# Streamed operands 64 bytes further along in SBUF, in an adaLN block with linear attention and a token mixer

## The chip, the cores and the metric

One core of a Trainium2 chip runs the whole program; the other cores are idle. The metric is the time of one execution on the device in microseconds; a profile is taken of one execution. The kernel is written in Bass with the Tile framework, in an order set by hand.

## The reference, cut to what matters

All tensors are float32: x is 2048 tokens by 448 channels, wqkv 448 x 1344, wo 448 x 448, w1 2048 x 1792, w2 1792 x 2048, w_mod 448 x 2688.

```python
mod = (_silu(c) @ w_mod).reshape(c.shape[0], 6, 1, -1)
sa, ca, ga, sb, cb, gb = (mod[:, i] for i in range(6))
h = _layernorm(x) * (1 + ca) + sa
q, k, v = heads of h @ wqkv                      # 16 heads of 28 channels
pq, pk = phi(q), phi(k)                          # elu + 1
o = (pq @ (pk^T v)) / (pq . sum of pk over tokens)
x = x + ga * (o @ wo)
h = _layernorm(_layernorm(x) * (1 + cb) + sb)
u = _gelu(einsum("bsd,sf->bdf", h, w1) + b1)     # first product over tokens
y = einsum("bdf,fs->bds", u, w2) + b2            # second product over tokens
x = x + gb * transpose(y)
```

(The lines are shortened; the heads' reshapes are written in words.)

## The kernel before, in words

TensorE takes two operands per matmul: the *held* one (weights, 128 columns, loaded ahead by a LDWEIGHTS) and the *streamed* one (here up to 448 columns). To keep float32 accuracy at the rate of fp32r, the kernel cuts each float32 operand into a high and a low part, both of type fp32r: `split` (L69) copies to the high part on ScalarE (L70) and subtracts it from the whole on VectorE (L71); in some places the low part is made on ScalarE and by an accumulating DMA from GpSimd's queue instead (`w_low_dma` L186, `low` L349, `PIECE_DMA` L219). A product is then three matmuls: high x high, high x low, low x high.

Nearly all tiles lie in two pools with places of 2048 bytes: `slots` (76 places, `slot` L60) and `tok` (25 places, `tslot` L63). A tile of 448 columns fills 1792 bytes of its place. The 14 tiles `uw`, 3584 bytes each, lie in a pool `uparts` (L793), which is opened where `tok` was, once that is closed. The places of slots, tok and uparts all begin at multiples of 128 bytes.

The stages, in the order in which TensorE works:

- **Modulation and input** (to about 18 us of the span): c and w_mod, first LayerNorm.
- **Tokens, first pass** (18 to 111 us), 16 tiles of 128 tokens. `project` (L299) makes K (`kp`) and, for some tiles, Q (`qp`): it holds slices of the transposed, normalised tile (hh, hl) and streams the parts of the weights, Whi and Wlo, which lie in tok. `a_outer` (L385) holds slices of the normalised tile (xh, xl) and streams pkh and pkl, the parts of phi(k) made in `a_pk_parts` (L369), into four accumulators `cacc`. V is never made: K^T h is multiplied by the V weights afterwards (`kvb`, L594).
- **Folded output weights** (L717): kvm x wo in float32 (`wp`), cut into Wph and Wpl, which lie in tok.
- **Attention output** (128 to 215 us): the loop at L728 does, for turn i, the transposes of tile i (`tq`), the output product of tile i-1 (`b_out` L647, twelve matmuls that stream Wph and Wpl), later Q projections, statistics and normalisation of tiles i-2 to i-4 on ScalarE, VectorE and GpSimd, and a first share of the first product over tokens. `b_norm2` (L692) and `b_low2` make H2h and H2l, the parts of the twice normalised tile.
- **First product over tokens** (`up`, 156 to 325 us): `step` (L709) and `acc3` (L704) hold slices of the parts of w1 (ph, pl) and stream H2h and H2l: L705 and L707 stream the high part, L706 the low one. `finish_u` (L804) applies gelu, and writes the parts of u into uw: in two halves of 224 columns, each as high then low. `u_parts` (L799) writes sums of u's halves into ordinary slots (`ut1` to `ut4`).
- **Second product over tokens** (325 us to the end): token tiles 0 to 9 are done by Strassen's scheme, seven products for four quadrants (`mult7` L877, out `y`): L889 streams 448 columns and L890 the first 224 of a uw or a ut tile. Three of the seven stream uw, four stream ut. Tiles 10 to 15 are done in the plain form (`mult1` L937, out `yp`), which uses `acc3` again and streams two pieces of 224 columns out of uw. The list `order` (L957) interleaves the two; loads and splits are called some entries ahead.

The order on each engine is the order in which the code is written (`manual_schedule`). DMAs go out on SyncE's queue, the accumulating ones on GpSimd's.

Of the kernel before, what the change touches and what calls it, by code (L numbers as in the profile page):

```python
# [8 lines left out]
F32 = mybir.dt.float32  # L9
F32R = mybir.dt.float32r  # L10
# [4 lines left out]
P = 128  # L15
S, D, F = 2048, 448, 1792
NT = S // P
NF = F // P
G = 112
# [23 lines left out]
def block_kernel(ctx: ExitStack, tc: tile.TileContext, x, wqkv, wo, w1, b1, w2, b2, c, wmod, out):  # L43
# [16 lines left out]
    def slot(name, w=D, dt=F32, parts=P):  # L60
        return slots.tile([parts, w], dt, name=name, tag="slot", padded_shape=[P, 512])

    def tslot(name, dt=F32, parts=P, w=D):  # L63
        return tok.tile([parts, w], dt, name=name, tag="tok", padded_shape=[P, 512])

    def bank(name):
        return psum.tile([P, 512], F32, name=name, tag="bank")

    def split(full, hi, lo):  # L69
        nc.scalar.activation(hi, full, AF.Copy)  # L70
        nc.vector.tensor_sub(lo, full, hi.bitcast(F32))  # L71
# [100 lines left out]
    Whi, Wlo = {}, {}  # L172

    def w_high(j, ch):
        Whi[j, ch] = tslot(f"wh{j}_{ch}", F32R)
        nc.scalar.activation(Whi[j, ch], raw_w[j, ch], AF.Copy)

    def w_low(j, ch):
        w, r = Whi[j, ch], raw_w[j, ch]
        if ch < 3:  # L180
            Wlo[j, ch] = tslot(f"wl{j}_{ch}", F32R)
            nc.vector.tensor_sub(Wlo[j, ch], r, w.bitcast(F32))
        else:
            nc.vector.tensor_sub(w[64:128], r[64:128], w[64:128].bitcast(F32))

    def w_low_dma(j, ch):  # L186
        w, r = Whi[j, ch], raw_w[j, ch]
        if ch < 3:
            Wlo[j, ch] = tslot(f"wl{j}_{ch}", F32R)
            lo, hi = Wlo[j, ch], w  # L190
        else:
            lo = hi = w[64:128]
            r = r[64:128]
        nc.scalar.activation(lo, hi.bitcast(F32), AF.Copy, scale=-1.0)
        nc.gpsimd.dma_start(lo, r, accum_op=ALU.add)
# [4 lines left out]
    raws, parts = {}, {}  # L200
# [148 lines left out]
    def low(t, lo, full, hi):  # L349
        if t in DVE_LOW:  # L350
            nc.vector.tensor_sub(lo, full, hi.bitcast(F32))
        else:
            nc.scalar.activation(lo, hi.bitcast(F32), AF.Copy, scale=-1.0)
            nc.gpsimd.dma_start(lo, full, accum_op=ALU.add)
# [13 lines left out]

    def a_pk_parts(t):  # L369
        pk = pkf.pop(t)  # L370
        hi, lo = slot(f"pkh{t}", dt=F32R), slot(f"pkl{t}", dt=F32R)
        nc.scalar.activation(hi, pk, AF.Copy)
        low(t, lo, pk, hi)
        if t in (0, 1, NT - 1):
            pksum.append(pk)
        elif t == NT - 2:
            pksum14.append(pk)
        else:
            nc.gpsimd.dma_start(pksum[t % 2], pk, accum_op=ALU.add)
        pks[t] = (hi, lo)  # L380
# [62 lines left out]
    a_first((2, 3))  # L443
    keep_warm(2)
    w_high(1, 0)
    a_copy((0, 1))
    a_copy((2,))
    a_copy((3,))
    del tps[0]
    st.pop(0)  # L450
    a_norm_a(1)
    w_high(1, 1)
    a_norm_b(1, sap[:, :D])
    a_dup(1)
    w_low(1, 0)
    w_high(1, 2)
    w_low(1, 1)
    kp0 = project0(1, "kp", lambda: a_transpose(1))
    a_split(1)
    w_high(1, 3)  # L460
    w_low(1, 2)
    w_low(1, 3)
    mod_out(0, sap)
# [3 lines left out]
    for ch in range(4):  # L467
        w_high(0, ch)
    a_exp(0, kp0)
    w_low_dma(0, 0)  # L470
    a_norm_b(2)
    w_low_dma(0, 1)
    a_stats(3)
    a_dup(2)
# [20 lines left out]
    a_exp(2, kp2)  # L495
    a_norm_b(4)
    a_pk_parts(0)
    a_dup(4)
    a_pk(2, kp2)
    a_phi_q()  # L500
    a_pk_parts(1)
    a_q(2)
    a_high(2)
# [6 lines left out]
    for t in range(3, NT):  # L510
# [15 lines left out]
        a_pk(t, kp)  # L526
        a_phi_q()
        a_pk_parts(t - 1)
        if t + 3 < NT:
            a_stats(t + 3)  # L530
# [14 lines left out]
        if t == 4:  # L545
            for g in range(4):
                w = tslot(f"wo{g}", parts=G)
# [58 lines left out]
    H2h, H2l = [None] * NT, [None] * NT  # L606
# [85 lines left out]
    def b_norm2(t, i):  # L692
        rs = rss[i - 1][:, 1:2]
        nb = small.tile([P, 1], F32, name=f"nb{t}", tag="nb")
        nc.gpsimd.tensor_mul(nb, nm2s.pop(t), rs)
        nc.scalar.activation(ys[t], ys[t], AF.Identity, bias=nb, scale=rs)
        H2h[t] = slot(f"h2h{t}", dt=F32R)
        H2l[t] = slot(f"h2l{t}", dt=F32R)
        nc.scalar.activation(H2h[t], ys[t], AF.Copy)

    def b_low2(t):
# [15 lines left out]
    for g in range(4):  # L717
        wp = bank(f"wp{g}")
        nc.tensor.matmul(wp[:G, :D], kvm[:, g * G:(g + 1) * G], wo_sb[g], start=True, stop=True)
        hi = tslot(f"wph{g}", F32R, G)  # L720
        lo = tslot(f"wpl{g}", F32R, G)
        split(wp[:G, :D], hi, lo)
        Wph.append(hi)
        Wpl.append(lo)
# [3 lines left out]
    for i in range(NT + LAG):  # L728
# [11 lines left out]
        t = i - LAG  # L740
# [19 lines left out]
        if norm2:  # L760
            b_norm2(i - 4, i)
# [28 lines left out]


    tok_ctx.__exit__(None, None, None)
    uparts = ctx.enter_context(tc.tile_pool(name="uparts", bufs=1, reuse_waits="tile"))  # L793
    HD = D // 2
    PAIRS, RS = NF // 2, ((0, 4), (4, 3))
# [195 lines left out]
    for o0, n in W1G[1:]:  # L991
# [5 lines left out]
        for r in range(first, NT):  # L997
# [4 lines left out]
            if xleft and k % 2:  # L1002
                t = xleft.pop(0)
# [13 lines left out]
    for n, (kind, p) in enumerate(order):  # L1017
        if jobs:
            jobs.pop(0)()
        while xleft:  # L1020
            t = xleft.pop(0)
# [40 lines left out]
```

## Time and profile before

| | |
|---|---|
| time, median of 3 runs | 458.64 us (458.63 to 460.37) |
| profiled execution, device time | 458.67 us |
| its span | 457.0 us |
| TensorE clock granted, mean | 1.00 |

In the profile, PE is TensorE's matmuls, PEld its weight loads (they run beside the matmuls), DVE VectorE, ACT ScalarE, POOL GpSimd, SP SyncE. A group of instructions has its line, engine, operation and `out<-in` by the program's tile names; a timeline row begins with start and duration in us; a row of a tile view gives minimum, median and maximum duration in ns, then the first and the last start. A row of the chain gives start and length of a piece of the chain of work that ended last. Matmuls overlap in the records: each lasts longer than the distance to the next one's start.

### The profile page before, as it was taken

Reading aid. Unit: us, or ns where it says so; the run is one execution under the profiler, and the core shown is the slowest. Engines: PE = TensorE matmul, PEld = TensorE weight load, DVE = VectorE, ACT = ScalarE, POOL = GpSimd, SP = SyncE. Lnnn points to the kernel's source line nnn. Section 1 sums busy time; section 2 is a strip of 40 time slices with the busy share of each in tenths; the row PEclk is TensorE's granted clock in tenths of the full one; section 3 lists DMA queues with packets and bytes.
Section 4 is the critical chain, followed back from the end, with each engine's and each line's share of the span. In section 5 each row is a group of like instructions: output and inputs, shape, how many; then the busy total and the mean of one; then the engine's idle time right before and its main releaser. Section 6 shows DMA issues by size and latency. Waiting matters only on the chain.

```text
span 457.0 us, 7265 instructions
## 1 busy us (share of the span) xinstructions
PE 451.6 (99%) x2378; PEld 409.9 (90%) x2378; DVE 356.7 (78%) x781; ACT 241.4 (53%) x538; POOL 90.9 (20%) x163
## 2 busy tenths in 40 slices
PE   8999999999999999999999999999999999999996
PEld 7689998998799999988999999999999999999996
DVE  5798897878898898896559676629696977798982
ACT  1648766635456576676665445226556262536350
POOL 2215675620014355554300000000000000000000
PEclk9999999999999999999999999999999999999999
DMA  8969999993200003222407453317960583628312
GB/s 228 287 174 174 172 193 227 210 226 116 70 1 2 23 24 103 61 47 48 126 17 230 162 193 106 112 39 227 288 187 23 177 239 113 176 99 250 112 55 98
DMA packets 60550, 61.85 MB, mean 135 GB/s; under 512 B 9248, under 2 KB 53856, under 8 KB 60512
## 3 DMA queue, kind: packets, MB, share of 16 engines
q1 hardware_dynamic: 54752, 52.45, 38.2%
q0 software_dynamic: 5760, 8.95, 12.0%
q8 instruction: 18, 0.29, 0.3%
q14 instruction: 20, 0.16, 0.1%
HBM read 45.09 MB, written 7.34 MB: 115 GB/s over the span
## 4 chain that ended last, share of the span: by engine, by line
PE 90%; ACT 3%; POOL 2%; DVE 1%; DMA 1%; issue 1%; SPq 1%; DVEq 0%
PE y L889 11%; PE up L705 9%; PE up L707 9%; PE up L706 9%; PE cacc L394 8%; PE kp L312 7%; PE qp L312 7%; PE y L890 5%; PE op L654 5%; PE yp L705 4%; PE yp L707 4%; PE yp L706 4%; PE tp L291 1%; DMA wm<-in_w_mod_dram 1%; PE tq L638 1%; PE modp L169 1%
## 5 line engine op out<-in xcount | busy, mean ns | idle before, releaser
L705 PE MATMUL up<-h2h,ph 128*128 128x448 f32 x224 | 82.2, 367 | 0.0
L706 PE MATMUL up<-h2l,ph 128*128 128x448 f32 x224 | 81.8, 365 | 0.0
L707 PE MATMUL up<-h2h,pl 128*128 128x448 f32 x224 | 81.8, 365 | 0.0
L71 DVE TENSOR_TENSOR pl<-pr,ph 128x512 fp32r<-128x512 f32 (+1 forms) x60 | 36.3, 615 | 13.0 <-ACT ph L70 8.3
L706 PEld LDWEIGHTS up<-h2l,ph 128*128 128x128 f32 x224 | 42.1, 188 | 3.5 <-issue 0.2
L705 PEld LDWEIGHTS up<-h2h,ph 128*128 128x128 f32 x224 | 42.1, 188 | 3.5 <-issue 0.2
L707 PEld LDWEIGHTS up<-h2h,pl 128*128 128x128 f32 x224 | 42.1, 188 | 3.4
L70 ACT ACTIVATE ph<-pr 128x512 fp32r<-128x512 f32 (+1 forms) x60 | 32.8, 567 | 16.3 <-PE up L706 11.4
L895 ACT ACTIVATE cc<-y 128x448 f32<-128x448 f32 x15 | 8.2, 545 | 56.5 <-PE y L890 39.8
L705 PE MATMUL yp<-uw,qw 128*128 128x448 f32 x84 | 31.1, 370 | 0.0
L707 PE MATMUL yp<-uw,qw 128*128 128x448 f32 x84 | 30.7, 366 | 0.0
L706 PE MATMUL yp<-uw,qw 128*128 128x448 f32 x84 | 30.7, 365 | 0.0
L394 PE MATMUL cacc<-pkh,xh 128*128 128x448 f32 x64 | 24.8, 387 | 0.0
L654 PE MATMUL op<-wph,pth 112*128 112x448 f32 x64 | 24.7, 386 | 0.0
L654 PE MATMUL op<-wpl,pth 112*128 112x448 f32 x64 | 23.4, 366 | 0.0
L394 PE MATMUL cacc<-pkl,xh 128*128 128x448 f32 x64 | 23.4, 366 | 0.0
L654 PE MATMUL op<-wph,ptl 112*128 112x448 f32 x64 | 23.4, 365 | 0.0
L70 ACT ACTIVATE qw<-q 128x256 fp32r<-128x256 f32 (+1 forms) x56 | 18.9, 352 | 7.7 <-DMA q<-in_B_w_dram 7.0
L312 PE MATMUL kp<-wh,hh 128*128 128x448 f32 x60 | 22.2, 375 | 0.0
L312 PE MATMUL qp<-wh,hh 128*128 128x448 f32 x60 | 22.2, 375 | 0.0
L810 DVE TENSOR_TENSOR u<-u,mod 128x448 f32<-128x448 f32 x14 | 8.7, 620 | 17.1 <-ACT u L809 17.1
L642 ACT ACTIVATE pth<-tq 112x512 fp32r<-112x512 f32 x16 | 9.6, 599 | 23.4 <-PE tq L638 20.4
(198 smaller groups left out, 1242.0 us busy)
## 6 DMA issues: line engine op xcount, KB each, us to landing
pr<-in_B_w_dram SPq DMA_DIRECT2D x48, 256.0 KB, 2.9
a<-in_B_w_dram SPq DMA_DIRECT2D x20, 256.0 KB, 5.2
wm<-in_w_mod_dram SPq DMA_DIRECT2D x24, 196.0 KB, 4.6
a<-in_B_w_dram SPq DMA_DIRECT2D x20, 192.0 KB, 4.9
x<-in_A_x_dram SPq DMA_DIRECT2D x16, 224.0 KB, 4.5
xpark<-x SPq DMA_DIRECT2D x16, 224.0 KB, 1.9
q<-in_B_w_dram SPq DMA_DIRECT2D x28, 128.0 KB, 3.2
xb<-xpark SPq DMA_DIRECT2D x16, 224.0 KB, 4.3
```

The source lines that it names most:

```text
L70: nc.scalar.activation(hi, full, AF.Copy)
L71: nc.vector.tensor_sub(lo, full, hi.bitcast(F32))
L312: nc.tensor.matmul(o, a[:, ch * P:(ch + 1) * P], b, start=(n == 0), stop=(n == 10))
L394: nc.tensor.matmul(cacc[ch][:, :D], a[:, s], b, start=(t == 0 and i == 0), stop=(t == NT - 1 and i == len(todo) - 1))
L642: nc.scalar.activation(phs[t][0], tps[t][:G, :], AF.Copy)
L654: nc.tensor.matmul(opb[t][:, :D], a[:, s], b, start=(n == 0), stop=(n == 11))
L705: nc.tensor.matmul(ps[:, :D], hi[:, sl], mh, start=first, stop=False)
L706: nc.tensor.matmul(ps[:, :D], hi[:, sl], ml, start=False, stop=False)
L707: nc.tensor.matmul(ps[:, :D], lo[:, sl], mh, start=False, stop=last)
L810: nc.vector.tensor_mul(u, u, mods[5])
L889: nc.tensor.matmul(ps[:, :D], h[:, s], w, start=opens and r == 0, stop=False, skip_group_check=True)
L890: nc.tensor.matmul(ps[:, :HD], l[:, s], w[:, :HD], start=False, stop=closes and r == PAIRS - 1, skip_group_check=True)
```

## The change

A helper `moving` takes a place of 512 columns and hands out columns 16 to 464 of it, so that the 448 columns begin 64 bytes into the place. All tiles that fp32r matmuls stream out of slots and tok come from it now: the parts of the QKV weights, of phi(k), of the twice normalised tiles and of the folded output weights. Ahead of the pool of the uw tiles a pool with one unused tile of 64 bytes is opened, so that every uw tile stands 64 bytes further as well. The ut tiles of `u_parts` and all held operands stay where they are. No instruction is added; the diff in full:

```diff
@@ -63,6 +63,10 @@
     def tslot(name, dt=F32, parts=P, w=D):
         return tok.tile([parts, w], dt, name=name, tag="tok", padded_shape=[P, 512])
 
+
+    def moving(new, name, dt=F32R, parts=P):
+        return new(name, dt=dt, parts=parts, w=512)[:, 16:16 + D]
+
     def bank(name):
@@ -172,13 +176,13 @@
     def w_high(j, ch):
-        Whi[j, ch] = tslot(f"wh{j}_{ch}", F32R)
+        Whi[j, ch] = moving(tslot, f"wh{j}_{ch}")
         nc.scalar.activation(Whi[j, ch], raw_w[j, ch], AF.Copy)
 
     def w_low(j, ch):
         w, r = Whi[j, ch], raw_w[j, ch]
         if ch < 3:
-            Wlo[j, ch] = tslot(f"wl{j}_{ch}", F32R)
+            Wlo[j, ch] = moving(tslot, f"wl{j}_{ch}")
             nc.vector.tensor_sub(Wlo[j, ch], r, w.bitcast(F32))
@@ -186,7 +190,7 @@
     def w_low_dma(j, ch):
         w, r = Whi[j, ch], raw_w[j, ch]
         if ch < 3:
-            Wlo[j, ch] = tslot(f"wl{j}_{ch}", F32R)
+            Wlo[j, ch] = moving(tslot, f"wl{j}_{ch}")
             lo, hi = Wlo[j, ch], w
@@ -368,7 +372,7 @@
     def a_pk_parts(t):
         pk = pkf.pop(t)
-        hi, lo = slot(f"pkh{t}", dt=F32R), slot(f"pkl{t}", dt=F32R)
+        hi, lo = moving(slot, f"pkh{t}"), moving(slot, f"pkl{t}")
@@ -694,8 +698,8 @@
-        H2h[t] = slot(f"h2h{t}", dt=F32R)
-        H2l[t] = slot(f"h2l{t}", dt=F32R)
+        H2h[t] = moving(slot, f"h2h{t}")
+        H2l[t] = moving(slot, f"h2l{t}")
         nc.scalar.activation(H2h[t], ys[t], AF.Copy)
@@ -717,8 +721,7 @@
-        hi = tslot(f"wph{g}", F32R, G)
-        lo = tslot(f"wpl{g}", F32R, G)
+        hi, lo = moving(tslot, f"wph{g}", parts=G), moving(tslot, f"wpl{g}", parts=G)
         split(wp[:G, :D], hi, lo)
@@ -790,6 +793,8 @@
     tok_ctx.__exit__(None, None, None)
+    uspace = ctx.enter_context(tc.tile_pool(name="uspace", bufs=1, reuse_waits="tile"))
+    uspace.tile([P, 16], F32, name="uspace")
     uparts = ctx.enter_context(tc.tile_pool(name="uparts", bufs=1, reuse_waits="tile"))
```

## The prediction

> **What bounds the kernel now.** I read the page's busy times first, then the chain that ended last, then single matmuls in the timeline.
>
> ```profile
> span 457.0 us, 7265 instructions
> PE 451.6 (99%) x2378; PEld 409.9 (90%) x2378; DVE 356.7 (78%) x781; ACT 241.4 (53%) x538; POOL 90.9 (20%) x163
> ...
> PEclk9999999999999999999999999999999999999999
> ...
> PE 90%; ACT 3%; POOL 2%; DVE 1%; DMA 1%; issue 1%; SPq 1%; DVEq 0%
> ```
>
> TensorE is busy 99% of the span at full granted clock and holds 90% of the chain. So the time is a sum over matmuls of the distance from one start to the next, and only something that changes that distance moves the end. The durations in the groups are longer than that distance, because matmuls are pipelined. The timeline of the first product over tokens (every line from 299.99 to 305.87 starts one matmul; 30 distances between these two and the one before) shows the distance itself:
>
> ```profile
> 299.79 0.36 PE L707 MATMUL up<-h2h,pl 128*128 128x448 f32 x1
> 299.99 0.36 PE L705 MATMUL up<-h2h,ph 128*128 128x448 f32 x1
> ...
> 305.87 0.36 PE L707 MATMUL up<-h2h,pl 128*128 128x448 f32 x1
> ```
>
> (305.87 - 299.79) / 30 = 0.2027 us for a stream of 448 columns. The chain, merged by line, shows more than one such pace, for the same eleven matmuls of the K projection in two neighbouring token tiles, and the float32 matmuls that make the folded output weights:
>
> ```profile
> 51.11 2.23 PE kp L312 x11
> ...
> 60.95 2.27 PE kp L312 x11
> ```
> ```profile
> 120.44 3.01 PE wp L719 x8
> ```
>
> 2.23 / 11 = 0.203, 2.27 / 11 = 0.206, 3.01 / 8 = 0.376. Instructions, shapes and places in SBUF modulo 2048 bytes are the same in the two kp rows; only the phase in which they follow what came before differs. A distance that has two steady values for the same work is what two streams that disturb each other would give. The float32 stream of the same 448 columns needs 0.376; if fp32r runs at twice its rate, 0.188 would be its undisturbed distance, and 0.0147 us of each 0.2027 is something else. What runs beside every matmul is the load of the next weights.
>
> ```profile
> 195.33 0.36 PE L706 MATMUL up<-h2l,ph 128*128 128x448 f32 x1
> 195.53 0.36 PE L707 MATMUL up<-h2h,pl 128*128 128x448 f32 x1
> ...
> 195.97 0.13 PEld L638 LDWEIGHTS tq<-ident,pn 128*112 128x112 f32 x1 [0.45 <-issue]
> ```
>
> The L707 at 195.53 is one of the few with no load beside it: the next one starts at 195.97, when its stream is over. Its own group, alone in the window 195.75 to 195.85, and the group of all L707 (mean in ns behind the comma):
>
> ```profile
> L707 PE MATMUL up<-h2h,pl 128*128 128x448 f32 x1 | 0.4, 360 | 0.0
> ```
> ```profile
> L707 PE MATMUL up<-h2h,pl 128*128 128x448 f32 x224 | 81.8, 365 | 0.0
> ```
>
> 360 against 365 ns: with the load beside it a stream is 5 ns longer. No other row prices the load, and I found three such matmuls in all. A second one speaks against it: the very last matmul of the kernel (plain form, no load after it), beside its group:
>
> ```profile
> L707 PE MATMUL yp<-uw,qw 128*128 128x448 f32 x1 | 0.4, 367 | 0.0
> ```
> ```profile
> L705 PE MATMUL yp<-uw,qw x84: 365/368/380, 324.9 to 452.5; 128*128 128x448 f32 x84
> L706 PE MATMUL yp<-uw,qw x84: 363/365/367, 325.1 to 452.7; 128*128 128x448 f32 x84
> L707 PE MATMUL yp<-uw,qw x84: 363/366/367, 325.3 to 452.9; 128*128 128x448 f32 x84
> ```
>
> 367 alone against a median of 366.
>
> **The change, part by part.** It adds no instruction and moves none. Slots and tok tiles are 2048 bytes apart and both pools begin at a multiple of 128 bytes; u's 3584-byte parts begin where tok began. So today every streamed operand and every weight tile of the fp32r matmuls stand a multiple of 128 bytes from each other. Afterwards the streamed one stands 64 bytes further.
>
> How many streams this reaches, from the loops: 165 kp and 165 qp (11 for each of 15 tiles), 176 cacc (11 x 16), 192 op (12 x 16), 672 up (three rows of 224), 252 yp (three of 84), and of the Strassen form the 3 of 7 products that stream uw, 35 each at L889: 105. Together 1727 streams of 448 columns. The other 140 stream ut, which u_parts keeps in plain slots; they stay.
>
> What one of them gains is shown by no row, since no fp32r pair stands 64 bytes apart. The bounds: 14.7 ns (0.2027 down to 0.188), nothing, and a loss of 3.6 ns (2.27 - 2.23 over 11, if the shift put all streams into the slower phase). I take 5 ns, the lone row, as if the shift removed what the load costs; for yp I take nothing, since its lone row shows 367. So (1727 - 252) x 5 ns = 7.4 us.
>
> [...]
>
> The short matmuls (L890, 224 columns) count nothing:
>
> ```profile
> 336.14 0.27 PE L890 MATMUL y<-uw,a11l 128*128 128x224 f32 x1
> 336.24 0.38 PE L889 MATMUL y<-uw,a11h 128*128 128x448 f32 x1
> 336.46 0.26 PE L890 MATMUL y<-uw,a11l 128*128 128x224 f32 x1
> ```
>
> L889 starts 0.10 us after L890 and shows 0.38 instead of 0.36: its weights began to load with L890 and are late, so a shorter L890 would only lengthen the wait. Bounds: 0 to 105 x 5 ns = 0.5 us.
>
> Not all of it is paid. In the attention-output stage the chain leaves TensorE:
>
> ```profile
> 175.57 0.76 ACT y L696
> ...
> 179.83 0.94 POOL pl L223
> ...
> 201.84 0.95 POOL pl L223
> ...
> 206.26 0.54 DVE pn L627
> ```
> ```profile
> 160.00:195.00 35.00, 35.00 (x185) 32.17 (x184) 30.73 (x73) 24.29 (x52) 18.98 (x40) 1.00 0.24 61
> ```
>
> From 175.57 to 206.80 the statistics, splits and accumulating DMAs of each token tile hand on to the next, and TensorE only keeps up (the figures behind the window's length are PE, PEld, DVE, ACT and POOL: DVE is busy 30.73 of 35 us). Six turns of 24 shifted matmuls lie there: 144 x 5 ns = 0.7 us are not gained, since pn would be as late as now. If this chain takes over in the whole stage (366 shifted streams from 128.5 us on), 1.8 us are lost.
>
> The writers of the shifted tiles (L70 on ACT, L71 on DVE, the accumulating DMAs on POOL's queue) write the same bytes; I cost them at nothing. Their cover: TensorE's own work, and for pkl the three tiles by which cacc follows. A DMA into pkl lands after 3.8 us,
>
> ```profile
> DMA to landing us min/median/max: 3.1/3.8/7.1
> ```
>
> and without that cover each microsecond more would be a microsecond of TensorE. The unused tile has no writer. uw3, uw7 and uw11 now reach 64 bytes into one more old tok tile (ph10, pd15, wph0), a wait for readers long gone: uw is first written at 237.1, and wph is last streamed at 214.1.
>
> ```profile
> L70 ACT ACTIVATE uw<-u x14: 558/579/581, 237.1 to 328.0; 128x448 fp32r<-128x448 f32 x14
> ```
> ```profile
> L654 PE MATMUL op<-wph,pth x64: 362/368/457, 128.5 to 214.1; 112*128 112x448 f32 x64
> ```
>
> Sum: -7.4 + 0.7 = -6.7 us. The profiled execution took 458.67 (span 457.0 and 1.67 around it), practically the median of 458.64; 458.67 - 6.7 = **452.0 us**.
>
> **The rivals.**
>
> *Nothing happens: 458.7.* For it: places that are multiples of 128 bytes apart make no difference now. L706 of yp streams from 896 bytes further into uw than L705 and L707 and lies in the same 363 to 367. And tq holds slices of pn 448 bytes apart, half of them 64 bytes off the identity that is streamed, with
>
> ```profile
> L638 PE MATMUL tq<-ident,pn x64: 270/272/295, 123.3 to 207.3; 128*112 128x128 f32 x64
> ```
>
> a median of 272 and a minimum of 270: no sign of two kinds. Against it: these stream float32 at half the rate, where 0.376 leaves room. [...]
>
> *Slower.* The shift changes the phase between stream and load, and the phase of the second kp row (0.206) becomes the rule. 1727 x 3.6 ns = 6.2 us: 464.9. Its place is every fp32r stream, and it decides as soon as the mean distance in up rises by 1.3 ns (0.5% of 458.7 us over 1727). For it: that phase exists and holds for whole runs of matmuls. Against it: 0.203 is much the commoner today, with no care for the phase.
>
> *The whole excess goes: about 439.* 14.7 ns x 1727 = 25.4 us, less the 366 streams of the attention-output stage (5.4 us), where the other engines would then set the pace. Against it: the lone matmul at 360 ns is nowhere near 14.7 ns shorter than 365. [...]
>
> *It only reaches part of the streams* lies inside the forecast's own range: half of 6.7 gives 455.3.
>
> **How the numbers follow.** Forecast 0.40 (own range 448 to 456), whole excess 0.07, nothing 0.28, slower 0.25. A difference under about 0.5% (2.3 us) can hardly be told from no change here. Faster by more than that: 0.40 + 0.07 = 0.47; within it 0.28; slower 0.25. For 8 in 10 the range leaves out the 0.07 of the whole excess and the far end of the slower case (over 466): 444 to 466.
>
> **What would show it.** Right: the median of L705 to L707 of up near 360 ns and thirty distances taking 5.9 instead of 6.08 us; kp and qp rows of the chain at 2.17 for eleven; y streaming ut unchanged while y streaming uw is shorter. Nothing: the same 365. Slower: medians of 369, eleven in 2.27 everywhere. The stage from 175 to 207 should keep its 31 us, with TensorE waiting for pn more often. The prediction is wrong if durations change by another amount than 5 ns, if yp changes where I count nothing, or if a wait on SP, ACT or DVE appears behind uw.

## The result: 2.0 us less, a third of the forecast's gain

| | median | lowest to highest | runs |
|---|---|---|---|
| before | 458.76 us | 458.63 to 460.37 | 6 |
| after | 456.75 us | 455.93 to 457.06 | 6 |

After divided by before is 0.994, 95% interval 0.9922 to 0.9959. So the kernel became 0.6% faster; the forecast had 6.7 us less (452.0), the range 444 to 466. The profiled execution of after took 457.06 us, its span 455.3.

The page of after, the lines that answer to those of before (all lines of code stand 4 further down in `acc3` and `project`: L705 to L707 are now L709 to L711, L312 is L316, L394 is L398; L889 and L890 are L894 and L895):

```profile
span 455.3 us, 7265 instructions
...
PE 448.9 (99%) x2378; PEld 409.9 (90%) x2378; DVE 356.6 (78%) x781; ACT 241.7 (53%) x538; POOL 91.6 (20%) x163
...
PE 80%; POOL 4%; ACT 4%; DVE 4%; DMA 3%; issue 3%; SPq 1%; POOLq 0%; DVEq 0%
```

The same 7265 instructions. TensorE still fills 99% of the span, but its share of the chain fell from 90% to 80%: other engines took over for some 10%. Both halves of that are the result in small: matmuls follow one another faster, and part of what they gained is waited away.

The timeline of the first product over tokens shows the faster part (every line from 296.84 to 302.64 starts one matmul; 30 distances between the first and the last row):

```profile
296.64 0.36 PE L711 MATMUL up<-h2h,pl 128*128 128x448 f32 x1
296.84 0.36 PE L709 MATMUL up<-h2h,ph 128*128 128x448 f32 x1
...
302.64 0.36 PE L711 MATMUL up<-h2h,pl 128*128 128x448 f32 x1
```

6.00 us in place of 6.08: 200.0 ns from start to start in place of 202.7. The change does what its words say, and one shifted stream gains **2.7 ns**.

Where the profiled execution lost and gained, by stage, from the starts of the stages' first matmuls (us; the attention output is counted to the start of its last `op`; the last column is 2.7 ns times the shifted streams of the stage, and a turn that ran at 206.7 ns before could give more):

| stage | before | after | difference | possible |
|---|---|---|---|---|
| start, to the first kp on split weights | 17.16 | 18.09 | +0.93 | 0 |
| tokens, first pass | 95.86 | 95.39 | -0.47 | -1.10 (407 streams) |
| kvb, folded weights, attention output | 100.38 | 99.69 | -0.69 | -1.14 (423) |
| first product (after the attention output) | 110.40 | 108.97 | -1.43 | -1.46 (540) |
| second product | 128.02 | 128.09 | +0.07 | - |

The start is not put down to the change: in both chains it hangs on a load of w_mod, which took 5.68 us in the profile of before and 6.61 in that of after, and in the eleven profiles of the block in this study the start lies between 16.93 and 18.09 us in no order that follows their code. Without it, the stages gained 2.5 us in this one execution.

Two stages kept less than was possible. The chain of waits of after, in the first pass (start, length, what), below the shares of the chain of before from 40 to 95 us, which is TensorE's alone:

```profile
by line: PE kp L312 43.8%; PE cacc L394 42.6%; PE tp L291 8.7%; PE qp L312 4.0%; PE modp L169 1.4%
```
```profile
46.83 2.20 PE kp L316 x11
...
61.38 2.21 PE kp L316 x11
63.59 0.45 PE tp L295 x4
...
64.51 0.72 POOL rs L272
...
66.58 7.55 DMA pkl<-pk
...
74.18 1.89 PE cacc L398 x8
...
76.12 0.89 POOL rs L272
...
91.15 0.54 DVE wo L560
91.69 0.61 DVE hl L75
...
92.34 2.08 PE kp L316 x9
```

Up to 64 us eleven `kp` take 2.20 to 2.21 in place of 2.23 to 2.27, and TensorE sets the pace. From there to 92 us, GpSimd and its queue, VectorE and a transfer into pkl do. In the attention output, `tq` now waits for pn (the row of the waits of PE: us in total, times, longest), which it did not before:

```profile
PE tq L642 <- DVE pn L631: 0.6, 2, 0.4
```

### The profile page after: what moved, and what is told of

It is laid out like the page before. It is cut to its first block, busy times and chain, and to the rows that moved or that the text cites. A ratio compares the mean times of both kernels' runs of the same rounds, so it can differ in the third digit from the quotient of the medians.

```text
span 455.3 us, 7265 instructions
## 1 busy us (share of the span) xinstructions
PE 448.9 (99%) x2378; PEld 409.9 (90%) x2378; DVE 356.6 (78%) x781; ACT 241.7 (53%) x538; POOL 91.6 (20%) x163
## 4 chain that ended last, share of the span: by engine, by line
PE 80%; POOL 4%; ACT 4%; DVE 4%; DMA 3%; issue 3%; SPq 1%; POOLq 0%; DVEq 0%
PE y L894 11%; PE up L711 8%; PE up L710 8%; PE up L709 8%; PE qp L316 7%; PE y L895 6%; PE cacc L398 5%; PE kp L316 5%; PE yp L709 4%; PE yp L711 4%; PE yp L710 4%; PE op L658 4%; DMA pkl<-pk 2%; DMA wm<-in_w_mod_dram 1%; ACT y L700 1%
## 5 line engine op out<-in xcount | busy, mean ns | idle before, releaser
L711 PE MATMUL up<-h2h,pl 128*128 128x448 f32 x224 | 81.3, 363 | 0.0
L709 PE MATMUL up<-h2h,ph 128*128 128x448 f32 x224 | 81.1, 362 | 0.0
L709 PEld LDWEIGHTS up<-h2h,ph 128*128 128x128 f32 x224 | 41.9, 187 | 3.1 <-issue 0.2
L711 PEld LDWEIGHTS up<-h2h,pl 128*128 128x128 f32 x224 | 42.0, 188 | 2.4
L709 PE MATMUL yp<-uw,qw 128*128 128x448 f32 x84 | 31.2, 371 | 0.0
L711 PE MATMUL yp<-uw,qw 128*128 128x448 f32 x84 | 30.6, 365 | 0.0
L398 PE MATMUL cacc<-pkh,xh 128*128 128x448 f32 x64 | 24.6, 385 | 0.0
L398 PE MATMUL cacc<-pkl,xh 128*128 128x448 f32 x64 | 23.3, 363 | 0.2 <-DMA pkl<-pk 0.2
L316 PE MATMUL kp<-wh,hh 128*128 128x448 f32 x60 | 22.0, 371 | 0.0
L316 PE MATMUL qp<-wh,hh 128*128 128x448 f32 x60 | 21.9, 371 | 0.0
L75 DVE TENSOR_TENSOR qw<-q,qw 128x256 fp32r<-128x256 f32 (+1 forms) x56 | 18.9, 352 | 3.8 <-ACT qw L74 3.8
L316 PE MATMUL kp<-wh,hl 128*128 128x448 f32 x60 | 21.7, 366 | 0.1
```

The source lines that it names most:

```text
L316: nc.tensor.matmul(o, a[:, ch * P:(ch + 1) * P], b, start=(n == 0), stop=(n == 10))
L398: nc.tensor.matmul(cacc[ch][:, :D], a[:, s], b, start=(t == 0 and i == 0), stop=(t == NT - 1 and i == len(todo) - 1))
L709: nc.tensor.matmul(ps[:, :D], hi[:, sl], mh, start=first, stop=False)
L711: nc.tensor.matmul(ps[:, :D], lo[:, sl], mh, start=False, stop=last)
```

## The experiments

Three theories stood against each other. **Distance**: what matters is how many bytes lie between the place that is streamed and the place whose weights are loaded. **Load**: the weight load costs the running stream time, and 64 bytes spare it that (the forecast's 5 ns). **Rounding of the phase**: the change only moved instructions against each other, and 200.0 is one more steady phase, whatever the bytes.

### bench_offsets: TensorE alone, the offset as the only variable

A kernel of matmuls only: 26 sections of 48, each with three matmuls per slice in the kernel's own rhythm. It leaves out the block's whole computation. One section streams 448 columns from `off` floats into a tile; tiles lie multiples of 2048 bytes apart, and the slices of weights in them multiples of 512.

```python
a = w[:, hoff + i * 128:hoff + i * 128 + held]
b = st[:, off:off + cols]
nc.tensor.matmul(ps[:held, :cols], a, b, start=(k == 0), stop=(k == n - 1))
```

> Only TensorE works: sections of 48 fp32r matmuls, each of which loads 128 columns of weights (hi, hi, lo in turn) and streams 448 columns of one tile; the output is not the reference's (zeros and copies of x). Sections oa to ok stream from 0, 8, 16, 32, 48, 64, 80, 96, 112, 128 and 256 bytes past a multiple of 512, with the weights at a multiple of 512. Theory A (the distance between the two reads decides): oa about 0.2027 us from start to start as in the kernel before, of (64 bytes) about 0.2000; ha (weights 64 bytes on, stream at 0) like of, hb (both 64 bytes on) like oa. Theory B (where the stream itself begins decides): ha like oa, hb like of. Theory C (the load plays no part): wa to wd, with 64 and 32 weight columns in place of 128, have the pace of oa and of; if the load is the cause, wc is nearer to 0.197. ta and tb, two pieces of 224 columns as the plain form streams them: 0.2027 in both if the plain form gains nothing by itself; tb 0.2000 if it only seemed so in the kernel. na, nb: 224 columns, half of 0.2027.

The chain, one row for each section (0, 8, 16, 64 and 256 bytes; then the weights 64 bytes on with the stream at 0, and both 64 bytes on; last the 64 bytes again):

```profile
16.72 9.73 PE oa L52 x48
26.45 9.91 PE ob L52 x48
36.35 9.62 PE oc L52 x48
...
65.52 9.61 PE of L52 x48
...
114.42 9.90 PE ok L52 x48
124.32 9.70 PE ha L52 x48
134.02 9.91 PE hb L52 x48
...
252.18 9.60 PE off L52 x48
```

Divided by 48: 202.7, 206.5, 200.4, **200.2** at 64 bytes, 206.3 at 256, and 200.0 when the 64 bytes came back at the end. The steady paces (the last 30 distances of a section) are 202.7, 206.7, 200.0, 200.0 and 206.7; 32 bytes gave 204.5, 48 gave 203.0, 80 gave 203.3, 96 gave 205.3, 112 gave 206.7 and 128 gave 204.0. So of the eleven places only 16 and 64 bytes reach 200.0. Two things follow. The offset alone sets a pace between 200.0 and 206.7, with the same instructions and no other engine at work, so the rivals "nothing" and "slower" are out as mechanisms for these streams. And both operands moved by 64 bytes (`hb`, 206.7) is as bad as neither: it is the distance that counts. The theory had one miss: with the weights 64 bytes on and the stream at 0 (`ha`) it expected 200.0, and the pace was 202.2, so the direction of the distance counts too. The section at 0 once more (`oaa`) gave 206.7, so distance 0 has two steady paces; one order of sections could not separate that from the phase, and the next bench was made for it.

### no_uspace and h2_only: parts of the change

```diff
-    uspace = ctx.enter_context(tc.tile_pool(name="uspace", bufs=1, reuse_waits="tile"))
-    uspace.tile([P, 16], F32, name="uspace")
```

> The change without the unused tile, so that uw stays where it was. Theory A and the trace after (distances in the second product unchanged, total gain at its begin 1.64 us and at its end 1.61): the same time as the changed kernel, 456.7, ratio 0.995 to 0.996. If the unused tile costs or gains by itself, the times differ by more than 0.5 us.

456.68 us, ratio 0.9952 (0.9931 to 0.9972): the same as with the unused tile. The end of the plain form, the last 36 `yp` of the kernel, shows that the tile does act, and there against the kernel. The timeline, 30 distances to the last matmul, of after and then of before:

```profile
445.20 0.36 PE L711 MATMUL yp<-uw,qw 128*128 128x448 f32 x1
...
451.33 0.37 PE L711 MATMUL yp<-uw,qw 128*128 128x448 f32 x1
```
```profile
446.84 0.37 PE L707 MATMUL yp<-uw,qw 128*128 128x448 f32 x1
...
452.94 0.37 PE L707 MATMUL yp<-uw,qw 128*128 128x448 f32 x1
```

6.13 us against 6.10, 204.3 ns against 203.3; without the tile it is 203.3 again. The second product as a whole took 128.02 us without the tile, as in before, against 128.09 with it: less than the totals can tell.

The other part: before, with only the twice normalised tiles moved.

```diff
-        H2h[t] = slot(f"h2h{t}", dt=F32R)
-        H2l[t] = slot(f"h2l{t}", dt=F32R)
+        H2h[t] = moving(slot, f"h2h{t}")
+        H2l[t] = moving(slot, f"h2l{t}")
```

> The kernel before with only the twice normalised tiles (H2h, H2l) 64 bytes on: 672 streams x 2.7 ns = 1.8 us less, of which the turns before 207 us (some 130 streams) may keep nothing: 457.0 to 457.4. Theory that the first pass gives the gain: 458.7. Up at 0.2000 from start to start, kp, qp, cacc and op as before at 0.2027.

457.5 us, ratio 0.9971 (0.9957 to 0.9985). The first product fell from 110.40 to 108.96, as in after, and the attention output stayed at 100.20; the other stages moved by no more than 0.43 us of scatter. So more than half of the result is `up` alone. From 217 to 322 us the chain of before and that of after hold nothing but `up`, although VectorE works for 69.6 of these 105 us beside it.

### bench_phases: the same offsets entered in four phases

Before each section a short float32 matmul of another length shifts the rhythm (40 matmuls per section).

```python
nc.tensor.matmul(kps[:, :n], sf[:, :P], sf[:, :n], start=True, stop=True)   # n = 40, 68, 96, 124
section(...)
```

> TensorE alone again (output zeros and copies of x, not the reference's). Each kind of section comes four times, every time behind one float32 matmul of another length, so that it starts in another phase. z: stream and weights at multiples of 512 bytes; s: stream 64 bytes on; q: stream 16 bytes on; h: weights 64 bytes on; b: both 64 bytes on. Theory A (distance between the two reads): s and h at 0.2000 each time, z and b at 0.2027 or 0.2067. Theory B (where the stream begins): s and b at 0.2000, z and h above. Theory D (only the phase decides, the place does nothing): every kind shows the same mixture of 0.2000, 0.2027 and 0.2067. [...] p, g (twice each): two pieces of 224 columns, 448 or 464 columns apart, 64 bytes on: 0.2033 and 0.2000 as in the run before. ea, eb: 8 weight columns: 0.197 or less if the load's length is the cause, 0.2027 to 0.2067 if it is not.

The chain rows of the third phase: stream at 0, at 64 and at 16 bytes, the weights 64 bytes on, and both:

```profile
100.22 8.14 PE zc L52 x40
...
108.58 8.01 PE sc L52 x40
...
116.79 8.04 PE qc L52 x40
...
125.03 8.12 PE hc L52 x40
...
133.36 8.12 PE bc L52 x40
```

The steady paces over all four phases: 0 bytes 202.7 four times; 64 bytes 200.0 four times; 16 bytes 202.2, 200.0, 200.0, 202.2; weights 64 bytes on 202.2 four times; both moved 206.7 once and 202.7 three times. The phase theory fell: 64 bytes gives 200.0 from each of the four phases. The phase picks between 202.7 and 206.7 when the distance is 0 (here with both moved; the two `kp` rows of before show the same pair) and between 200.0 and 202.2 at 16 bytes. The direction of the distance counts again: 64 bytes the other way gives 202.2.

The same bench shortened the stream at distance 0, with weights of 32 columns: 512 columns 231.7 ns, 384 173.3, 320 143.3, 256 117.8 and 192 88.4. From the longest to 256 that is (231.7 - 117.8) / 256 = 0.445 ns for a column, and 1 to 4 ns are left beside it: nearly all of the 202.7 goes with the number of columns, not with a fixed gap. The line is rough, and at 64 bytes it is another one (231.7 for 512 columns and 113.3 for 256, 0.463 ns for a column).

### off16: 16 bytes in place of 64

```diff
-        return new(name, dt=dt, parts=parts, w=512)[:, 16:16 + D]
+        return new(name, dt=dt, parts=parts, w=512)[:, 4:4 + D]
```

> The changed kernel with 16 bytes in place of 64 for slots and tok (uw stays 64 on). Theory that any step off the common grid will do (section oc of the run before: 0.2000): the same as the changed kernel, 456.7, up at 0.2000. Theory that it needs 64 bytes: up back at 0.2027 and the time back at 458.5.

458.19 us, ratio 0.9978 (0.9966 to 0.999). `up` runs at 200.0, but eleven `kp` or `cacc` take 2.20 in some turns and 2.22 to 2.24 in others, and the attention output kept its 100.40. The granted clock of this profile reads 0.95 from start to end; as `up` keeps its 200.0 under it, the clock does not explain the slower rows. They are what a bench with two paces at 16 bytes would give: 64 is the more robust distance.

### bench_plain: what the load costs, and why the plain form does not gain

Sections of 36, each after a phase shift. The first ten vary the columns held (128, 96, 64, 32, 8), at 0 and at 64 bytes. The other eight imitate the plain form: the second matmul of three streams from 896 bytes further on (`other`), in two pieces of 224 columns or in one.

```python
o = off + (other if m == 1 else 0)
b = st[:, o:o + 896].rearrange("p (h d) -> p h d", h=2)[:, :, :224]   # or st[:, o:o + D]
```

> TensorE alone (output not the reference's). Sections la to le stream 448 columns at distance 0 behind weights of 128, 96, 64, 32 and 8 columns, ma to me the same at 64 bytes, each in two phases (last letter). Theory that the weight load steals 5 ns from each stream at distance 0: the distance from start to start falls from 0.2027 towards 0.1977 as the load gets shorter. Theory that only the timing against the load matters: 0.202 to 0.2067 at any width, no steady fall. Sections xa, ya stream as the plain form does (two pieces of 224 columns, high, low, high, weights hi, hi, lo in one tile) at 0 and 64 bytes; xb, yb always the high part; xc, yc in one piece with the same alternation; xd, yd in one piece without it. Kernel's own tails: 0.2033 and 0.2044, so xa 0.2033 and ya 0.2044. If the two pieces are what spoils the 64 bytes, yc and yd show 0.2000; if it is the alternation between parts 896 bytes apart, yb shows less than ya and yc as much as ya.

The tile views of the first and the fifth section in their second phase, loads (minimum, median and maximum in ns):

```profile
L52 PEld LDWEIGHTS lab<-st,hi x24: 187/188/192, 152.5 to 159.3; 128*128 128x128 f32 x24
```
```profile
L52 PEld LDWEIGHTS leb<-st,hi x24: 87/88/91, 182.5 to 189.2; 128*8 128x8 f32 x24
```

and the chain: 128 and 8 columns held at 0 bytes in the first phase and in the second; 128, 32 and 8 at 64; then the plain form at 64, in two pieces without the step of 896 bytes, in one piece with the step, and in one piece without it:

```profile
17.36 7.51 PE laa L52 x36
...
47.40 7.28 PE lea L52 x36
...
152.76 7.33 PE lab L52 x36
...
182.68 7.29 PE leb L52 x36
...
190.15 7.25 PE mab L52 x36
...
212.49 7.43 PE mdb L52 x36
...
220.10 7.40 PE meb L52 x36
...
265.55 7.41 PE ybb L73 x36
...
273.14 7.41 PE ycb L73 x36
...
280.72 7.25 PE ydb L73 x36
```

At distance 0 the load fell from 188 to 88 ns. The steady pace (last 30 distances) fell with it from 202.7 to 202.2 in the second phase and from 206.7 to 202.3 in the first. That first fall is no price of the load's length: it came with the first step, 202.7 with 96 columns, which 128 columns have in the other phase, and 64, 32 and 8 columns then share 202.2 to 202.3 in both phases. No section came near the 197.7 that a stolen 5 ns would have left. **The load theory, as a price by length, fell.** The load still matters: at 64 bytes the pace is 200.0 with 128 columns held, 202.2 with 96, 201.8 to 201.9 with 64 and 206.7 with 32 (`mdb`), with 8 206.7 and 206.0 in the two phases. The good distance is good for this length of load only.

In the plain form the pace at 64 bytes is 204.2 to 204.5 with the step of 896 bytes, in two pieces or in one, close to the 204.3 of the kernel's tail. In two pieces without the step it is 203.3 in one phase and 204.4 in the other (`ybb`); in one piece without it 200.0. So each of the two, the step between high and low parts and the second piece, spoils the 64 bytes by itself.

### uw_gap: 64 bytes also between the two halves of a uw tile

```diff
-            uw[f] = uparts.tile([P, 4 * HD], F32R, name=f"uw{f}")
+            uw[f] = uparts.tile([P, 4 * HD + 16], F32R, name=f"uw{f}")
...
+        return [bass.AP(w.tensor, w.offset + o, [list(w.ap[0]), [D + 16, 2], [1, HD]]) for o in (0, HD)]
```

> The changed kernel with 16 columns left free between the two halves of each uw tile, so that the plain form's two pieces of 224 columns are 464 columns apart and the second one, too, keeps the step of 64 bytes that the first has (sections tb and td of the run before: 0.2032 and 0.2000). Theory that the piece's second start spoils the plain form: yp falls from 0.2033 to 0.2000, 252 x 3 ns = 0.7 us less than the changed kernel: 456.0. Theory that the plain form's stream is limited otherwise: 456.7.

457.44 us, ratio 0.996 (0.9946 to 0.9974). The tail runs at 203.0, yet the second product took 128.39 us, 0.30 more than in after: a pair of the long and the short Strassen matmul that stream uw went from 314.9 to 317.6 ns (mean distance from one short one to the next), which over 105 pairs is 0.28 us. The edit does more than was meant. A uw tile grows from 3584 bytes, a multiple of 512, to 3648, and the tiles lie one behind the other; so each begins 64 bytes further than the one before it on the 512-byte grid of the weights, and only two of the fourteen still begin at 64. The run therefore tests neither theory. The benches do: two pieces 464 columns apart ran at 200.0 as long as all streams took the same part (bench_offsets, bench_phases), against 203.3 for pieces 448 columns apart, but with the step of 896 bytes even one piece runs at 204.5 (bench_plain). A plain form without the step was not run in the kernel.

### lag4 and before_lag4: cacc one tile later

If the transfer into pkl is what TensorE meets in the first pass, a further tile of lag should free the gain there. The same edit was made to no_uspace and to before.

```diff
-KV_LAG = 3
+KV_LAG = 4
```

(with a guard for the first tiles, and the last of them after the loop)

> The change without the unused tile, and the outer product of the first pass runs four tiles behind the projections in place of three, so that its operands have some 5 us more to arrive. Theory that part of the gain of the first pass is eaten by new waits there (1.4 us more in five matmuls between 38 and 91 us than before): most of what the operands of cacc cost (0.5 us at 72 us) comes back, those of kp (0.9 us at 85 and 91 us) only if they hang on the same queue: 455.7 to 456.3 against 456.7 without. Theory that these waits are not on the path, or move elsewhere: 456.7 or more.

> The kernel before with the same longer lag and nothing else. Before, TensorE hardly waits in the first pass (0.3 us at 75 and 91 us), so both theories expect 458.5 to 459; if the lag itself gives or costs more than 0.5 us, it can't be used to read the run beside it.

459.39 us (0.9998, 0.998 to 1.0016) and 461.28 (1.0044, 1.0026 to 1.0061). The pair differs by 1.9 us, much as without the lag, and the first pass by 98.20 against 99.26. But the lag itself costs 2.2 to 3.4 us in this pass (98.20 against 96.01, 99.26 against 95.86), at whose start TensorE now waits for ScalarE (the waits of lag4's weight loads):

```profile
PEld kp L316 <- ACT hh L74: 2.1, 1, 2.1
```

A control that moves by more than the effect decides nothing, so the pair is inconclusive.

### no_sum and before_no_sum: GpSimd's queue with less in it

The accumulating transfers that sum phi(k) over tokens are dropped, in no_uspace and in before. This leaves out part of the sum for the denominator; nothing else changes.

```diff
-        else:
-            nc.gpsimd.dma_start(pksum[t % 2], pk, accum_op=ALU.add)
```

> The change without the unused tile, and without the accumulating DMAs that add the tiles of phi(k) for the denominator (L379, eleven issues on GpSimd's queue), so the sum over tokens is that of a few tiles only. Theory that GpSimd's queue and what hangs on it hold up the first pass of the changed kernel: from the first kp on split weights to kvb, 94.7 to 95.2 us against 96.0 with them, and the wait for pkl at 72 us goes. Theory that the waits come from the last link alone (VectorE's own list of work): the pkl wait goes, those for hl (1.4 us) stay: 95.5.

> The kernel before without the same DMAs. If they cost nothing there: first pass 95.6 to 95.9 us as before (95.9), so that the difference to the run beside it (0.5 to 1.2 us) is the gain of the shorter streams that the waits had hidden.

455.62 us (0.9929, 0.9902 to 0.9956) and 458.5 (0.9984, 0.9967 to 1.0). In the totals the pair differs by 2.9 us where no_uspace and before differed by 2.4: not enough to argue from. The stage is clearer. The first pass took 94.44 against 95.49: **-1.05 us, nearly the 1.10 that 407 streams can give**. With the transfers the same two took 96.01 and 95.86. Each figure is one profile, and the first pass scatters: after, no_uspace and uw_gap run the same code there and took 95.39, 96.01 and 95.68, before and h2_only 95.86 and 96.09. Every pairing of these gives 0.7 us or less, and the 94.44 lies below all of them. The chains, no_sum and then before_no_sum, lie on TensorE to the end of the pass:

```profile
81.11 2.20 PE kp L316 x11
...
90.82 2.20 PE kp L316 x11
```
```profile
81.42 2.27 PE kp L312 x11
...
91.26 2.23 PE kp L312 x11
```

### wo_early: VectorE's scaling of wo at another place of the turn

In the chain of no_uspace, as in that of after, `wo` stands on VectorE just before hl, for which `kp` waits. The scaling was moved from the end of the turn to after `a_exp`.

```diff
+        if 11 <= t < 15:
+            nc.vector.tensor_mul(wo_sb[t - 11], wo_sb[t - 11], mods[2][:G])
...
-        if 11 <= t < 15:
-            nc.vector.tensor_mul(wo_sb[t - 11], wo_sb[t - 11], mods[2][:G])
```

> The change without the unused tile; the scaling of the four wo tiles on VectorE stands between the two halves of the normalisation, where VectorE waits 0.5 us for GpSimd, and no longer at the end of each turn ahead of the next hl. Nothing is left out. Theory that hl is late because of it: the waits of kp for hl at 85 and 91 us (two of the three, about 1.0 us) go, first pass 95.0 us, time 455.6 to 456.0. Theory that another link is as late: less than 0.4 us gained on 456.7.

456.38 us, ratio 0.9943 (0.9922 to 0.9964), first pass 95.16. The waits of the weight loads between 30 and 110 us, no_uspace and then wo_early:

```profile
PEld kp L316 <- DVE hl L75: 1.4, 3, 0.6
PEld cacc L398 <- DMA pkl<-pk: 0.5, 1, 0.5
```
```profile
PEld kp L316 <- DVE hl L75: 0.5, 2, 0.2
PEld tp L295 <- DVE h L283: 0.4, 1, 0.4
...
PEld cacc L398 <- DMA pkl<-pk: 0.3, 2, 0.2
```

The wait for hl fell from 1.4 to 0.5 us, and a wait of `tp` for h of 0.4 us appeared. 456.38 is the lowest median of a version that computes all of the block, but its interval covers that of no_uspace and of after: it can't be called faster than either.

## Why the prediction was right or wrong, point by point

- **What bounds the kernel.** Right. The time is a sum over TensorE's distances from start to start, the distances changed, and the end moved.
- **Two steady paces for the same work are two streams that disturb each other.** Borne out by the benches in this form: at distance 0 the phase picks 202.7 or 206.7, at 64 bytes with 128 columns held there is only 200.0, and both the place of the weights (202.2 with them 64 bytes on) and the number of columns loaded (206.7 at 64 bytes with 32 held) change the pace of the stream. What in the memory makes the distance count, no run shows.
- **What one stream gains: this step failed.** "I take 5 ns, the lone row, as if the shift removed what the load costs". The gain is 2.7 ns, a little over half. The step had two parts: that the load costs the stream a fixed 5 ns, and that the shift removes just this. The lone `up` at 360 ns was no price of the load: cutting the load by 100 ns left the pace at 202.2, and not near 197.7, and the same matmul in after, again with nothing beside it, reads (its group, alone in a window of the lines)

```profile
L711 PE MATMUL up<-h2h,pl 128*128 128x448 f32 x1 | 0.4, 367 | 0.0
```

  longer than the 363 that its group has from 195 to 206 us. The second lone row, 367 of `yp`, had said so; the forecast quoted it and used it for `yp` alone. The two lone records of `up` differ by 7 ns in the direction opposite to the pace. What the shift does is to move the pace from 202.7 to 200.0 by the distance of the two places. With 2.7 ns, the forecast's own sum would have been 1475 x 2.7 = 4.0 us.
- **Which streams.** Nearly right. 1370 of the 1475 counted gained (or could). The 105 L889 that stream uw did not: their pairs went from 314.1 to 314.9 ns. The forecast had seen that L889's weights come late there (their load takes 0.19 us from L890's start, and L889 starts 0.10 us after L890), and still paid it 5 ns (0.5 us).
- **`yp` at nothing.** Right in the sum: the second product took 128.09 against 128.02. The reason was another than the lone row: the plain form's pace moves under the shift, from 203.3 to 204.3 in the tail. It streams in two pieces, and every third stream lies 896 bytes on; in bench_plain each of these alone takes the 200.0 away (203.3 and 204.4 in two pieces without the step, 204.2 to 204.5 with the step).
- **The attention-output stage, 0.7 us not gained.** Right, at its price. 144 streams at 2.7 ns are 0.39 us; of 1.14 possible 0.69 came, so 0.45 are missing, and `tq` waits for pn as said. The stretch kept its length, as the forecast had named for a sign: from the start of the y at 175.57 us to that of the pn that ends the stretch it took 30.61 us in before, and between the same two instructions 30.62 in after. The trace has 390 shifted streams from 128.5 us on, not 366, so the bound would have been 1.95 us and not 1.8; it did not come into play.
- **Cover of the first pass: what was missed.** The writers of the shifted tiles were costed at nothing, with TensorE's own work as cover. Those on ScalarE and VectorE did not become slower (pkh 580 ns on ScalarE and pkl 619 on VectorE in after, 581 and 618 in before). The accumulating DMA into pkl took a median of 4.2 us to land against 3.8, at the longest 7.6 against 7.1; that no_sum had a median of 4.3 and kept its gain speaks against this as the cause, but whether the shift lengthens it is not settled. What gave way was the cover: TensorE would have come up to 1.1 us earlier, and GpSimd's queue, VectorE and the transfer into pkl stood less than that ahead of its need. Some 0.6 us were waited away in the profile of after, and all of it in that of no_uspace (96.01). no_sum gives it back, in one profile. Which of the three is met first differs from run to run (64 to 92 us in the chains), and wo_early moved only one of them.
- **The rivals.** For "nothing" speaks that the length of the load took nothing from the stream at distance 0: in bench_plain the load fell from 188 to 88 ns, and 64, 32 and 8 columns held share 202.2 to 202.3. That the place makes no difference does not agree: in bench_phases 202.7 at 0 bytes against 200.0 at 64, from each of the four phases, with nothing changed but an address; and of the multiples of 128 bytes, which the forecast took for alike, 128 gave 204.0 and 256 gave 206.7 (bench_offsets). "Slower" exists at 8 and at 256 bytes (206.7), not at 64 with 128 columns held. "The whole excess" fell: no distance that was tried gave 448 columns less than 199.9, and by the lengths of bench_phases nearly all of the time goes with the columns. Its 188 ns, half of the 376 of the float32 stream, was the author's estimate; no fp32r stream of 448 columns here reaches it, and what fills the 12 ns stays open.
- **The sum.** 2.7 ns x 1370 = 3.7 us; less 0.6 in the first pass and 0.45 in the attention output, and next to nothing in the second product, is 2.5 to 2.6 for the profiled execution without its late start, and 2.0 in the medians. Why the medians give 0.5 less than the stages of this one profile is not settled. The first pass scatters by 0.2 to 0.6 us between profiles of the same code, and no_uspace, against the 18 runs of before beside it (median 459.06), is 2.4 us faster.

## What to carry to other kernels

Measure a distance from start to start over thirty matmuls before you price anything in nanoseconds on TensorE; a single matmul's recorded duration varied by 7 ns for reasons other than the one it was read for. When TensorE is made faster everywhere, price each stage by what stands closest behind it: here the stage whose chain was TensorE's alone, before and after, kept 98% of its gain, and the two others about 40 and 60%. An offset that helps one shape of stream and load (448 columns in one piece and always from the same place in its tile, 128 held) has to be tried anew for another.

## What the runs showed of the hardware that was not expected

- With no engine at work but TensorE, the place of the streamed operand against the weights moves an fp32r matmul of 448 columns between 200.0 and 206.7 ns: 202.7 at 0 bytes (206.7 in another phase), 206.7 at 8, 200.0 at 64, 206.7 at 256, and 202.2 with the weights 64 bytes ahead instead.
- 64 bytes is good with loads of 128 columns (200.0) and bad with loads of 32 (206.7) or 8 (206.0 to 206.7), so a shorter load can make the same stream slower. No run explains it.
- Of 224 columns with 128 held, one matmul takes 111.5 ns, not half of 202.7: the chain of bench_offsets has

```profile
231.55 5.35 PE na L52 x48
```

  5.35 / 48 = 0.1115 us.
